# One transfer with an outermost dimension of two, replaced by two of 64 partitions

## The chip, the cores and the metric

The kernel runs on one core of a Trainium2 chip. What is measured is the device time of one execution in microseconds. A kernel is timed in several runs; the median counts. One more execution is recorded by the hardware profiler, and all rows below come from that one.

## What is computed

Four sequences of 576 tokens and eight heads of 64 go through causal attention whose scores get a decay term, and the result goes through two feed-forward layers. Cut to what matters:

```python
scores = np.matmul(q, k.transpose(0, 1, 3, 2)) / np.sqrt(D)      # B=4, H=8, S=576, D=64
cum = np.cumsum(np.log(np.clip(f, 0.0001, 1.0)), axis=-1)
decay = cum[:, :, :, None] - cum[:, :, None, :]
scores = np.where(causal, -1000000000.0, scores + decay)
attn = softmax(scores)
x = np.matmul(attn, v)                    # to 2304 tokens x 512
h = x @ w_in;  x = (h * clip(h + 3, 0, 6) / 6) @ w_out       # first layer, d_ff = 2048
h = x @ w_in2; g = 0 if h <= -1, (h + 1)**2 / 4 in the middle, h if h >= 1
out = g @ w_out2                          # second layer
```

## The kernel before

Attention is cut into jobs. A job of kind "two" takes the first 256 queries of two heads of one sequence; the other 320 queries of a pair of heads are three jobs: two of kind "one" (one head, 256 queries) and one of kind "last". The last job is a tile of 128 partitions: partitions 0 to 63 hold the last 64 queries of the first head, partitions 64 to 127 those of the second. There are 16 such tiles. For each job `u_load` issues the transfers two jobs ahead (k into kraw, q into qraw, the decay rows into dec), `u_split` (one job ahead) lets GpSimd mask the diagonal block of the decay (L569 and L573 for a last tile) and ScalarE and VectorE split k and q into a high and a low part (kk, qh, ql), `u_scores` makes the scores (L630 for a last tile, L655 for the others), VectorE adds the decay and takes the maximum (L606), ScalarE takes the exponential (L612), `u_norm` finishes the sum on ScalarE (L674), and VectorE makes its reciprocal (L675) and the normalised rows (L684). `u_trans` transposes these on TensorE (L697), `u_out` multiplies with v (L739).

The cumulated logarithms lie in the DRAM tensor ncum, one row of 576 numbers for each of 32 heads. dec repeats rows of it over partitions: for jobs "one" and "two" one row over all 128 partitions (L555), for a last tile row r over 64 partitions and row r+1 over the other 64 (L506).

The feed-forward matmuls are mixed with attention. `moe_h` (L833) multiplies by w_in and applies the first function (L840, L841, then L400 and L408 split the result g); `moe_o` (L876) multiplies by w_out, and when a block of tokens is done its sums go through osb (L898, L900) to the DRAM tensor x2d (L902). Blocks 0 and 1 are worked on in two parts each or in one (`OPEN`), so block 0 leaves two partial sums in two tensors x2d, which `moe_x` adds up later. Weights come in raw (wraw, L433), are put together by ScalarE and VectorE (wr, L445 to L456, then L400 and L408) and kept in DRAM (wf, L465) for a second visit. The second layer's matmuls are L833 and L883.

All transfers are issued by SyncE's queue in one order. The order on every engine is written by the kernel itself: `graph` gives each instruction a cost and `schedule` lists, engine by engine, what could start first by these costs; `plan` ties the instructions together in that order. Each engine then works through its list in order. So a change in the number of transfers can move instructions on every engine.

Of the kernel before, what the change touches and what calls it, by code (L numbers as in the profile page):

```python
# [8 lines left out]
F32 = mybir.dt.float32  # L9
# [5 lines left out]
B, H, S, D = 4, 8, 576, 64  # L15
NT, DM, DFF = B * S, H * D, 2048
P = 128
NCH = DFF // P
KD = DM // P
T1 = (512, 512, 512, 256, 512)  # L20
T2 = (512, 512, 512, 512, 256)
NB = len(T1)
NB2 = NB + len(T2)
# [15 lines left out]

SLOTS = (9, 9)  # L40
OPEN = ((0, 0, 8), (1, 0, 8), (1, 8, 16), (0, 8, 16))
LOOK = 5
LAG = 2
GO = 0
# [1 line left out]
LATE = (1, 2.0, 2)  # L46
WRAW = 3
AHEAD = 60000
LEAD = (1, 1, 1, 1, 1, 1)


def plan_weights(visits, slots, more, lag):
# [300 lines left out]
def tile_kernel(  # L353
# [10 lines left out]
    nc = tc.nc  # L364
# [9 lines left out]
    moe = pool("moe", 2)  # L374
    dram = pool("dram", 1, DRAM)
# [10 lines left out]
    att = pool("att", 2)  # L386
    rawp = [att]

    x2d = [dram.tile([DM, NT if x == 0 else T1[0]], F32, name=f"x2d{x}") for x in range(2)]
    wf = [  # L390
        [dram.tile([P, 2, 4, P], F32, name=f"wf{c}_{x}") for x in range(2)]
        for c in range(NCH)
# [1 line left out]
    ncum = dram.tile([B * H, S], F32, name="ncum")  # L394
# [14 lines left out]


    steps = [(j, c) for j, a, e in OPEN for c in range(a, e)]
    for j in range(2, NB2):
        order = range(NCH) if j % 2 else range(NCH - 1, -1, -1)
        steps += [(j, (j >= NB) * NCH + c) for c in order]
    opens = [g for g in range(len(steps)) if g == 0 or steps[g - 1][0] != steps[g][0]]
    closes = [g - 1 for g in opens[1:]] + [len(steps) - 1]
    parts = {g: [steps[x][0] for x in opens[:n]].count(steps[g][0]) for n, g in enumerate(opens)}
    g7 = (NB - 1) * NCH
    where, loads = [], []
    for x in range(2):  # L420
        a, b = plan_weights([c for _, c in steps], SLOTS[x], (16 - SLOTS[x], g7), LAG * x)
# [49 lines left out]
    place, t0 = {}, 0  # L471
    for b, half in ORDER:
# [10 lines left out]
        t0 = place[b, half][1]  # L483
# [14 lines left out]
    def u_load(n):  # L498
        d = jobs[n]
        b, hs, kind, p = d["b"], d["hs"], d["kind"], d["p"]  # L500
        h, nh = hs[0], len(hs)
        r = b * H + h
        if kind == "last":

            d["dec"] = att.tile([P, S], F32, tag="dec", name="dec")
            nc.sync.dma_start(  # L506
                out=d["dec"], in_=ncum[r:r + 2, :].unsqueeze(1).to_broadcast([2, D, S])
            )
            return
        q0, nq, nk = (0, QA, QA) if kind == "two" else (QA, S - QA, S)  # L510
        d["nat"] = n < NATS
# [296 lines left out]
    def moe_x(j):  # L808

        t0, w = FROM[j], WIDTH[j]  # L810
        for k in range(KD):
            x = moe.tile([P, 2, 512], F32R, tag="xt", name="x2", bufs=XT)
            hi, lo = x[:, 0, 0:w], x[:, 1, 0:w]
            full = lo.bitcast(F32)
            if j == NB:
                full, more = (moe.tile([P, 512], F32, tag="wr", name=f"part{y}", bufs=2) for y in range(2))
            nc.sync.dma_start(out=full, in_=x2d[0][k * P:(k + 1) * P, t0:t0 + w])
            if j == NB:
                nc.sync.dma_start(out=more, in_=x2d[1][k * P:(k + 1) * P, t0:t0 + w])
                nc.vector.tensor_tensor(out=full, in0=full, in1=more, op=ALU.add)  # L820
            rounded("p", hi, full)
            rest("v", lo, full, hi)
            xt[j, k] = x
# [126 lines left out]
    n1 = NB * NCH  # L950
# [73 lines left out]
    weights_until(-1)  # L1024


    spans = [(0, 8, 1), (8, 32, 2)] + [(j * NCH, (j + 1) * NCH, j + 1) for j in range(2, NB)]
    cost = [sum(x[0] for x in seq[:n]) for n in range(len(seq) + 1)]
    due = [ends[group(min(j, NB - 1))] for _, _, j in spans]
    goal, n0 = [], pos  # L1030
    for x, (a, e, j) in enumerate(spans):

        n2 = 2 * (e - a)
        left = cost[-1] - cost[n0]
        share = cost[n0] + left * LEAD[x] * (part[e] - part[a]) / (part[g7] - part[a]) if e < g7 else cost[-1]
        aim = max(cost[due[x]], min(share, cost[due[x]] + AHEAD))
        aim = max(aim, cost[n0])
        for y in range(n2):
            goal.append(cost[n0] + (aim - cost[n0]) * (y + 1) / n2)
        while n0 < len(seq) and cost[n0] < aim - 1:  # L1040
            n0 += 1
# [73 lines left out]
```

## Time and profile before

| | |
|---|---|
| time, median of 3 runs | 1024.39 us (1022.07 to 1025.25) |
| the profiled execution: its time | 1025.11 us |
| its span, first to last instruction | 1023.4 us |
| granted TensorE clock, mean over the span | 0.978 of full speed |
| TensorE busy | 994.8 us (97%) |
| VectorE busy | 588.0 us (57%) |
| ScalarE busy | 529.6 us (52%) |
| GpSimd busy | 73.0 us (7%) |

A row of the timeline gives the start in microseconds from the span's start, the duration, the engine (PE is TensorE, PEld its weight loads, DVE VectorE, ACT ScalarE, POOL GpSimd, SPq the queue of SyncE), the line, the operation, output and inputs by name, the shape, the number of instructions in the row and, in brackets, how long the engine stood idle before the row and what ended that. A row of the windows gives for a stretch the length, the busy time of each engine with its number of instructions, then the granted clock, the share of the 16 DMA engines' time in use, and GB/s.

### The profile page before, as it was taken

What the parts mean: (1) busy time and instruction counts of PE and PEld (TensorE: products, weight loads), DVE (VectorE), ACT (ScalarE), POOL (GpSimd) and SP (SyncE); (2) the same over time, 40 slices, a digit from 0 to 9 for tenths busy, and PEclk for the clock granted to TensorE, in tenths of its full rate; (3) what the DMA queues carried; (4) which work ended last, traced back from release to release, by engine and by line L of the source; (5) the groups of instructions that cost most, each with busy time, mean ns of one, the idle gap of its engine ahead of it and who ended that gap; (6) DMA issues with size and microseconds to landing.
All of it is one profiled execution on the core that took longest, in us unless ns stands there. A gap on an engine that the chain in (4) does not pass through costs nothing.

```text
span 1023.4 us, 14617 instructions
## 1 busy us (share of the span) xinstructions
PE 994.8 (97%) x5002; PEld 800.6 (78%) x5002; DVE 588.0 (57%) x1390; ACT 529.6 (52%) x1208; POOL 73.0 (7%) x192
## 2 busy tenths in 40 slices
PE   7889999998999999999999999999999999999998
PEld 5457767876677777778998888878888888888897
DVE  5899876798655555455533669999322322322232
ACT  5889765675655554455532336565333333333343
POOL 1111110110010010000000000201000000000000
PEclk8689999998999999999999999999999999999999
DMA  6766477854466776326636325443100100000010
GB/s 175 213 184 186 130 233 245 284 162 134 100 204 204 243 232 180 111 66 184 233 125 250 124 76 192 176 154 113 42 1 19 48 1 1 27 20 1 1 43 20
DMA packets 69193, 131.39 MB, mean 128 GB/s; under 512 B 11520, under 2 KB 34560, under 8 KB 69120
## 3 DMA queue, kind: packets, MB, share of 16 engines
q1 hardware_dynamic: 69120, 130.47, 41.4%
q8 instruction: 39, 0.64, 0.3%
q14 instruction: 34, 0.28, 0.1%
HBM read 105.20 MB, written 25.24 MB: 127 GB/s over the span
## 4 chain that ended last, share of the span: by engine, by line
PE 80%; DVE 9%; DMA 6%; ACT 2%; issue 2%; SPq 0%; DVEq 0%; POOL 0%; ACTq 0%; POOLq 0%
PE hp L833 33%; PE o L876 17%; PE o L883 17%; PE av L739 4%; PE pt L697 4%; PE sc L655 3%; DMA wraw<-in_w 3%; DMA kraw<-in_k 2%; PE sc L630 2%; DVE wr L453 1%; DVE wr L456 1%; DVE w L408 1%; DVE prob L606 1%; ACT prob L612 1%; DVE wr L446 1%
## 5 line engine op out<-in xcount | busy, mean ns | idle before, releaser
L833 PE MATMUL hp<-xt,w 128*128 128x512 f32 (+1 forms) x960 | 232.6, 382 | 1.1 <-ACT xt L400 0.7
L876 PE MATMUL o<-g,w 128*128 128x512 f32 (+1 forms) x960 | 229.4, 378 | 1.4 <-DVE osb L900 1.4
L833 PE MATMUL hp<-x,w 128*128 128x512 f32 (+1 forms) x960 | 211.5, 368 | 0.5 <-ACT w L400 0.3
L883 PE MATMUL o<-w,g 128*128 128x512 f32 x864 | 210.1, 390 | 0.0
L833 PEld LDWEIGHTS hp<-x,w 128*128 128x128 f32 x960 | 169.2, 188 | 32.7 <-ACT w L400 0.7
L833 PEld LDWEIGHTS hp<-xt,w 128*128 128x128 f32 x960 | 167.0, 192 | 31.8 <-issue 2.4
L876 PEld LDWEIGHTS o<-g,w 128*128 128x128 f32 x960 | 166.0, 189 | 29.7 <-DVE osb L900 1.8
L883 PEld LDWEIGHTS o<-w,g 128*128 128x128 f32 x864 | 161.2, 188 | 32.7
L845 DVE SCALAR_TENSOR_TENSOR u<-hp,u 128x512 f32<-128x512 f32 (+1 forms) x80 | 50.9, 636 | 166.8 <-ACT u L844 166.7
L408 DVE TENSOR_TENSOR g<-u,g 128x512 fp32r<-128x512 f32 (+1 forms) x160 | 102.4, 640 | 56.7 <-ACT g L400 30.3
L400 ACT ACTIVATE g<-u 128x512 fp32r<-128x512 f32 (+1 forms) x160 | 94.5, 591 | 75.8 <-DVE u L845 47.1
L843 ACT ACTIVATE u<-hp 128x512 f32<-128x512 f32 (+1 forms) x80 | 44.3, 554 | 157.9 <-PE hp L833 157.8
L612 ACT ACTIVATE prob<-prob,mx 128x128 f32<-128x128 f32 (+4 forms) x144 | 83.4, 580 | 55.5 <-DVE mx L606 55.3
L841 DVE SCALAR_TENSOR_TENSOR u<-u,hp 128x512 f32<-128x512 f32 (+1 forms) x80 | 50.5, 631 | 90.4 <-ACT u L840 90.1
L840 ACT ACTIVATE u<-hp 128x512 f32<-128x512 f32 (+1 forms) x80 | 44.0, 550 | 90.8 <-PE hp L833 90.6
L697 PE MATMUL pt<-ident,prob 128*128 128x128 f32 (+1 forms) x400 | 71.8, 294 | 13.6 <-DVE prob L684 10.1
L606 DVE CUSTOM_DVE_ANT_0 prob<-sc,dec 128x256 f32<-128x256 f32 (+1 forms) x112 | 58.6, 534 | 37.3 <-PE sc L655 22.5
L400 ACT ACTIVATE pt<-pt 128x512 f32<-128x512 f32 (+3 forms) x160 | 63.4, 433 | 25.2 <-PE pt L697 24.7
L697 PEld LDWEIGHTS pt<-ident,prob 128*128 128x128 f32 (+1 forms) x400 | 51.1, 148 | 32.4 <-DVE prob L684 10.0
L400 ACT ACTIVATE w<-wr 128x512 fp32r<-128x512 f32 x64 | 40.3, 629 | 28.8 <-DVE wr L456 28.5
L739 PE MATMUL av<-pt,vv 128*64 128x320 f32 (+3 forms) x448 | 53.7, 382 | 0.7 <-ACT pt L400 0.7
L445 ACT ACTIVATE wr<-wraw 128x512 f32<-128x512 f32 x64 | 42.9, 670 | 20.8 <-DMA wraw<-in_w 10.2
(69 smaller groups left out, 865.6 us busy)
## 6 DMA issues: line engine op xcount, KB each, us to landing
wraw<-in_w SPq DMA_DIRECT2D x64, 512.0 KB, 4.9
w<-wf SPq DMA_DIRECT2D x40, 512.0 KB, 8.1
wf<-w SPq DMA_DIRECT2D x28, 512.0 KB, 8.7
dec<-ncum SPq DMA_DIRECT2D x45, 256.0 KB, 3.6
kraw<-in_k SPq DMA_DIRECT2D x64, 144.0 KB, 4.1
x2d<-osb SPq DMA_DIRECT2D x22, 256.0 KB, 3.1
vv<-in_v SPq DMA_DIRECT2D x16, 320.0 KB, 7.4
dec<-ncum SPq DMA_DIRECT2D x16, 288.0 KB
```

The lines of the kernel that those rows point to most:

```text
L400: nc.scalar.activation(out=out, in_=in_, func=AF.Copy)
L408: e.tensor_tensor(out=out, in0=in_, in1=hi.bitcast(F32), op=ALU.subtract)
L606: nc.vector.tensor_tensor_reduce(out=py[:, a:e], in0=s, in1=dc, scale=-0.125, scalar=mx[:, 2 * z:2 * z + 1] if x else 3.0e38, op0=ALU.add, ...
L612: nc.scalar.activation(out=py, in_=py, func=AF.Exp, scale=-1.0, bias=mx[:, 2 * z + x:2 * z + x + 1], accum_out=sm[:, z:z + 1],)
L697: nc.tensor.transpose(t[:nk, o:o + P], p[:, c:c + nk], ident)
L739: nc.tensor.matmul(t[y * D:(y + 1) * D, o:nq], lhsT=vv[:, y, c], rhs=rhs, start=c == 0, stop=c == nkc - 1,)
L833: nc.tensor.matmul(hp, lhsT=ws[:, a, k], rhs=x[:, bb, 0:w], start=(k == 0 and a == 0 and bb == 0), stop=(k == KD - 1 and bb == 1),)
L841: nc.vector.scalar_tensor_tensor(out=u, in0=u, scalar=6.0, in1=hp, op0=ALU.min, op1=ALU.mult)
L843: nc.scalar.activation(out=u, in_=hp, func=AF.Relu, bias=0.5, scale=0.5)
L845: nc.vector.scalar_tensor_tensor(out=u, in0=hp, scalar=1.0, in1=u, op0=ALU.max, op1=ALU.min)
L876: nc.tensor.matmul(o, lhsT=ws[:, a, k], rhs=gg[:, bb], start=(n and k % m == 0 and a == 0 and bb == 0), stop=(last and bb == 1 and k % m = ...
L883: nc.tensor.matmul(acc[j][k], lhsT=gg[:, bb, k * P:(k + 1) * P], rhs=ws[:, a].rearrange("p k n -> p (k n)"), start=(n and a == 0 and bb == ...
```

## The change

The transfer of the decay rows for a last tile, one instruction whose outermost dimension has the size two, becomes two instructions of 64 partitions each. The other edits put constants in place that are worked out from `OPEN`; the second x2d tensor becomes 1024 columns wide instead of 512.

```diff
 SLOTS = (9, 9)
 OPEN = ((0, 0, 8), (1, 0, 8), (1, 8, 16), (0, 8, 16))
+OPENED = 1 + max(j for j, _, _ in OPEN)
+HEAD = sum(T1[:OPENED])
+NPART = max(sum(x[0] == j for n, x in enumerate(OPEN) if n == 0 or OPEN[n - 1][0] != x[0]) for j in range(OPENED))
...
-LEAD = (1, 1, 1, 1, 1, 1)
...
-    x2d = [dram.tile([DM, NT if x == 0 else T1[0]], F32, name=f"x2d{x}") for x in range(2)]
+    x2d = [dram.tile([DM, NT if x == 0 else HEAD], F32, name=f"x2d{x}") for x in range(NPART)]
...
-    for j in range(2, NB2):
+    for j in range(OPENED, NB2):
...
             d["dec"] = att.tile([P, S], F32, tag="dec", name="dec")
-            nc.sync.dma_start(
-                out=d["dec"], in_=ncum[r:r + 2, :].unsqueeze(1).to_broadcast([2, D, S])
-            )
+            for y in range(2):
+                nc.sync.dma_start(out=d["dec"][y * D:(y + 1) * D], in_=ncum[r + y:r + y + 1, :].to_broadcast([D, S]))
             return
...
-            if j == NB:
-                full, more = (moe.tile([P, 512], F32, tag="wr", name=f"part{y}", bufs=2) for y in range(2))
+            n = 1 + part_of.get(j - NB, 0)
+            if n > 1:
+                full = moe.tile([P, 512], F32, tag="wr", name="part0", bufs=2)
             nc.sync.dma_start(out=full, in_=x2d[0][k * P:(k + 1) * P, t0:t0 + w])
-            if j == NB:
-                nc.sync.dma_start(out=more, in_=x2d[1][k * P:(k + 1) * P, t0:t0 + w])
+            for y in range(1, n):
+                more = moe.tile([P, 512], F32, tag="wr", name=f"part{y}", bufs=2)
+                nc.sync.dma_start(out=more, in_=x2d[y][k * P:(k + 1) * P, t0:t0 + w])
                 nc.vector.tensor_tensor(out=full, in0=full, in1=more, op=ALU.add)
...
-    spans = [(0, 8, 1), (8, 32, 2)] + [(j * NCH, (j + 1) * NCH, j + 1) for j in range(2, NB)]
+    fresh = [g for g in opens if parts[g] == 0 and g < n1] + [n1]
+    spans = [(a, e, j + 1) for j, (a, e) in enumerate(zip(fresh, fresh[1:]))]
...
-        share = cost[n0] + left * LEAD[x] * (part[e] - part[a]) / (part[g7] - part[a]) if e < g7 else cost[-1]
+        share = cost[n0] + left * (part[e] - part[a]) / (part[g7] - part[a]) if e < g7 else cost[-1]
```

The order moves at more places than the queue. On the other engines it is that of before up to about 140 us of the profile, differs here and there until about 305, and hardly after that. Line numbers in the changed kernel are one to four higher.

**First place: SyncE's queue around 279 us.** dec is the decay rows, wf a 512 KB write of weights kept for later, vv the values, x2d the sums of a finished block. Before:

```order
L526 DMA kraw<-in_k 64x576 x2
L506 DMA dec<-ncum 128x1x576
L539 DMA qraw<-in_q 128x256
L540 DMA qraw<-in_q 128x64
L465 DMA wf_0_98<-w_0_113 128x1024
L493 DMA vv<-in_v 128x2x320
L902 DMA x2d_78<-osb 128x512 x2
```

Now:

```order
L509 DMA dec<-ncum 64x576 x2
L467 DMA wf_0_98<-w_0_113 128x1024
L527 DMA kraw<-in_k 64x576 x2
L495 DMA vv<-in_v 128x2x320
L540 DMA qraw<-in_q 128x256
L541 DMA qraw<-in_q 128x64
L905 DMA x2d_78<-osb 128x512 x2
```

The decay rows are now two instructions and stand ahead of kraw, and the write of wf moved up to stand directly behind them.

**Second place: ScalarE and TensorE around 265 to 272 us**, a last tile (prob_3268, now prob_3274) and the two jobs before it. ScalarE before:

```order
L612 ACTIVATE prob_3236,sum<-prob_3236,mx 128x512
L400 ACTIVATE kk<-kraw 128x576
L674 ACTIVATE sum<-sum 128x2
L612 ACTIVATE prob_3268,sum<-prob_3268,mx 128x576
L674 ACTIVATE sum<-sum 128x1
L400 ACTIVATE qh<-qraw 128x384
L840 ACTIVATE u<-hp 128x512
```

ScalarE now:

```order
L613 ACTIVATE prob_3242,sum<-prob_3242,mx 128x512
L675 ACTIVATE sum<-sum 128x2
L613 ACTIVATE prob_3274,sum<-prob_3274,mx 128x576
L843 ACTIVATE u<-hp 128x512
L675 ACTIVATE sum<-sum 128x1
L402 ACTIVATE kk<-kraw 128x576
```

The conversion of kraw, which waits for a transfer, moved from ahead of the sum to behind both sums. TensorE at the same place, before:

```order
L630 MATMUL sc<-kk,ql 128x512 x2
L630 MATMUL sc<-kk,ql 128x64 x2
L833 MATMUL hp<-xt,w_8_121 128x512 x11
L697 MATMUL pt<-ident,prob_3139 128x128 x2
L697 MATMUL pt<-ident,prob_3236 128x128
```

TensorE now:

```order
L631 MATMUL sc<-kk,ql 128x512 x2
L631 MATMUL sc<-kk,ql 128x64 x2
L836 MATMUL hp<-xt,w_8_121 128x512 x5
L879 MATMUL o_1989<-g,w_5_127 128x512 x2
L698 MATMUL pt<-ident,prob_3145 128x128 x2
L879 MATMUL o_1989<-g,w_5_127 128x512
```

Between the scores and the first transposes (pt) stood eleven matmuls of a feed-forward layer, and now stand seven.

**Third place: VectorE and TensorE around 247 to 252 us**, again a last tile (prob_3008, now prob_3013) and the job before it (prob_2865 and prob_2976, now prob_2870 and prob_2981). VectorE before:

```order
L453 SCALAR_TENSOR_TENSOR wr<-wraw,wr 128x512
L408 TENSOR_TENSOR ql<-qraw,qh 128x384
L456 SCALAR_TENSOR_TENSOR wr<-wraw,wr 128x512
L675 RECIPROCAL rd<-sum 128x2
L606 ISA prob_3008,mx<-sc,dec 128x512
L606 ISA mx 128x1
L684 TENSOR_SCALAR prob_2865<-prob_2865,rd 128x384
L408 TENSOR_TENSOR w_6_128<-wr,w_6_128 128x512
L684 TENSOR_SCALAR prob_2976<-prob_2976,rd 128x512
```

VectorE now:

```order
L458 SCALAR_TENSOR_TENSOR wr<-wraw,wr 128x512
L844 SCALAR_TENSOR_TENSOR u<-u,hp 128x512
L607 ISA prob_3013,mx<-sc,dec 128x512
L607 ISA mx 128x1
L410 TENSOR_TENSOR w_6_128<-wr,w_6_128 128x512
L676 RECIPROCAL rd<-sum 128x2
L607 ISA prob_3013,mx<-sc,dm,mx 128x64
L607 ISA mx 128x1
L410 TENSOR_TENSOR xt<-av,xt 128x320
L685 TENSOR_SCALAR prob_2870<-prob_2870,rd 128x384
L685 TENSOR_SCALAR prob_2981<-prob_2981,rd 128x512
```

The normalisation of the two tiles that are transposed next now has u, the small piece of the last tile's scores and xt ahead of it. TensorE there, before:

```order
L876 MATMUL o_1989<-g,w_3_125 128x512
L876 MATMUL o_1990<-g,w_3_125 128x512 x3
L630 MATMUL sc<-kk,qh 128x64 x2
L630 MATMUL sc<-kk,ql 128x64 x2
L697 MATMUL pt<-ident,prob_2865 128x128
```

TensorE now:

```order
L836 MATMUL hp<-xt,w_6_119 128x512 x3
L631 MATMUL sc<-kk,qh 128x64 x2
L631 MATMUL sc<-kk,ql 128x64 x2
L836 MATMUL hp<-xt,w_6_119 128x512 x6
L698 MATMUL pt<-ident,prob_2870 128x128 x2
```

Nine matmuls of the next feed-forward step now stand ahead of these transposes; the matmuls o that stood there were moved ahead of the scores.

## Rows read from the trace of the kernel before

**Rows 1.** Windows: engines' busy time by stretch, then granted clock, DMA share, GB/s.

```profile
235.00:256.00 21.00, 16.95 (x69) 12.85 (x68) 16.75 (x40) 11.83 (x27) 2.15 (x7) 0.84 0.41 120
256.00:276.00 20.00, 17.53 (x93) 13.15 (x92) 12.16 (x38) 11.83 (x32) 2.10 (x9) 0.91 0.46 113
276.00:295.00 19.00, 17.64 (x91) 13.24 (x90) 9.51 (x24) 9.25 (x22) 0.62 (x3) 1.00 0.48 148
295.00:1010.00 715.00, 714.39 (x3606) 593.15 (x3605) 352.66 (x735) 324.54 (x668) 36.70 (x90) 1.00 0.33 106
```

**Rows 2.** Timeline of TensorE: its waits from 126 to 295 us, and a run.

```profile
137.65 0.33 PE L697 MATMUL pt<-ident,prob 128*128 128x128 f32 x1 [1.77 <-DVE prob L684]
...
240.66 0.63 PE L697 MATMUL pt<-ident,prob 128*128 128x128 f32 x4 [2.00 <-DVE mx L606]
...
251.26 0.96 PE L697 MATMUL pt<-ident,prob 128*128 128x128 f32 x4 [1.02 <-DVE mx L606]
...
266.39 2.78 PE L833 MATMUL hp<-xt,w 128*128 128x512 f32 x11
271.64 1.72 PE L697 MATMUL pt<-ident,prob 128*128 128x128 f32 x7 [2.47 <-DVE prob L684]
...
293.85 1.65 PE L876 MATMUL o<-g,w 128*128 128x512 f32 x6 [1.36 <-DVE osb L900]
```

**Rows 3.** Timeline of VectorE and ScalarE: waits ahead of those of TensorE.

```profile
136.03 0.69 DVE L606 CUSTOM_DVE_ANT_0 prob<-sc,dec 128x512 f32<-128x512 f32 x1 [2.41 <-DMA dec<-ncum]
...
239.13 0.66 ACT L445 ACTIVATE wr<-wraw 128x512 f32<-128x512 f32 x1 [4.79 <-DMA wraw<-in_w]
239.82 0.43 DVE L446 TENSOR_SCALAR wr<-wr 128x512 f32<-128x512 f32 x1 [1.94 <-ACT wr L445]
...
241.62 0.69 DVE L408 TENSOR_TENSOR w<-wr,w 128x512 fp32r<-128x512 f32 x1 [1.10 <-ACT w L400]
...
268.87 0.69 DVE L606 CUSTOM_DVE_ANT_0 prob<-sc,dec 128x512 f32<-128x512 f32 x1 [3.47 <-DMA dec<-ncum]
...
269.46 0.68 ACT L400 ACTIVATE kk<-kraw 128x576 fp32r<-128x576 f32 x1 [3.21 <-DMA kraw<-in_k]
...
293.10 0.69 DVE L900 TENSOR_SCALAR osb<-o 128x512 f32<-128x512 f32 x1 [2.11 <-DMA x2d<-osb]
```

**Rows 4.** Timeline: weights issued behind decay rows; decay rows issued, and first read.

```profile
229.29 0.40 SPq L433 DMA_DIRECT2D wraw<-in_w  x1
...
259.45 0.55 SPq L506 DMA_DIRECT2D dec<-ncum  x1
...
268.80 0.24 POOL L569 TENSOR_SCALAR_AFFINE_SELECT dm<-dec 128x64 f32<-128x64 f32 x1 [5.28 <-DMA dec<-ncum]
```

**Rows 5.** Groups by line: busy us, mean ns, idle us before and its releaser.

```profile
L569 POOL TENSOR_SCALAR_AFFINE_SELECT dm<-dec 128x64 f32<-128x64 f32 x16 | 4.0, 250 | 146.0 <-DMA dec<-ncum 146.0
```

**Rows 6.** The chain of waits: start us, length us, what.

```profile
262.02 7.34 DMA kraw<-in_k
...
286.21 6.77 DMA x2d<-osb
```

**Rows 7.** DMA issues of the whole run: count, KB each, median us to landing.

```profile
wraw<-in_w SPq DMA_DIRECT2D x64, 512.0 KB, 4.9
...
dec<-ncum SPq DMA_DIRECT2D x45, 256.0 KB, 3.6
kraw<-in_k SPq DMA_DIRECT2D x64, 144.0 KB, 4.1
x2d<-osb SPq DMA_DIRECT2D x22, 256.0 KB, 3.1
```

**Rows 8.** DMA issues of the first 126 us alone.

```profile
kraw<-in_k SPq DMA_DIRECT2D x6, 144.0 KB, 2.9
```

**Rows 9.** Windows: the microsecond after the decay rows of 259.45 began to move.

```profile
261.00:262.00 1.00, 1.00 (x13) 0.77 (x10) 0.88 (x3) 1.00 (x5) 0.00 (x0) 1.00 0.18 54
```

**Rows 10.** Line L526: duration ns min/median/max, first and last start us.

```profile
L526 SPq DMA_DIRECT2D kraw<-in_k x80: 471/587/650, 9.0 to 479.6; - x80
```

## Prediction

> **What bounds the kernel now.** I read the windows first. TensorE is the engine that works almost all the time, so what the change can give is what TensorE loses while it waits or runs at the lower clock. From 295 to 1010 us it loses nothing: 714.39 busy of 715.00 at a granted clock of 1.00 [rows 1]. Whatever ends earlier before 295 therefore ends the program earlier by as much. Between 126 and 295, where the transfers that are changed are issued, TensorE is idle in four places: 1.77 us at 137.65 [rows 2], and by the windows 4.05 in 235:256, 2.47 in 256:276 and 1.36 in 276:295, together 9.65 us. Twice the clock falls behind such a stop, from 1.00 to 0.84 over 21 us and to 0.91 over 20 us; since the lower level is half of the higher (1.2 against 2.4 GHz), the share that is missing is time lost: 0.16 x 21 = 3.4 and 0.09 x 20 = 1.8 us [rows 1]. All that can be won is 9.65 + 5.2 = 14.9 us.
>
> The timeline then says who stops TensorE [rows 2]: the transposes L697 wait for VectorE at 137.65, 240.66, 251.26 and 271.64, and the second layer of matmuls L876 at 293.85. One step further back [rows 3] stand transfers. At 136.03 and 268.87 VectorE itself sat idle 2.41 and 3.47 us until the decay rows of a last tile had landed. At 239.13 ScalarE had waited 4.79 us for raw weights, and VectorE 1.94 and 1.10 us behind it. At 269.46 ScalarE had waited 3.21 us for kraw; at 293.10 VectorE 2.11 us for a write of x2d.
>
> These five have one thing in common. The decay rows of a last tile are issued at 259.45 and used at 268.80, 9.35 us later [rows 4]; over all 16 of them GpSimd stood 146.0 us, 9.1 each, waiting for them [rows 5]. And a transfer issued just behind one is late too: the weights issued at 229.29 [rows 4] reach ScalarE at 239.13, 9.8 us, where 4.9 is the median; kraw takes 7.34 us at 262.02 against a median of 4.1, x2d 6.77 at 286.21 against 3.1 [rows 6, 7]. While the decay rows travel almost alone, the queue moves 54 GB/s [rows 9]: 288 KB at that rate take 5.5 us, and 0.18 x 16 is about three DMA engines at work. So the one transfer uses a few of the sixteen engines, and what follows waits on those few.
>
> The Trainium skill, "DMA: Bandwidth & Descriptors", section "Rules for kernel authors", says that an outermost dimension smaller than 16 confines a transfer to at most that many engines; the 54 GB/s agree with it. The same section speaks against this change: two transfers to disjoint halves of the partitions are not worth the trouble, since both spread over the same engines and one follows the other; one transfer of 128 partitions is advised. By that rule alone the halves would land no earlier and the time would stay at 1024.4. The trace has the case that decides between them: 64 partitions x 576, 144 KB, as kraw, landed in 2.9 us before the first of the slow transfers [rows 8].
>
> **The parts, costed.** *Two transfers for one.* Sixteen instructions become 32. A 64-partition issue takes 0.587 us of the queue [rows 10], so what is queued behind (vv, raw weights, the next kraw) is issued up to 0.6 us later, at most 9.4 us of queue in all. For the weights behind the one at 228.6 this is 229.3 + 0.6 + 4.9 = 234.8, against 239.13 now; ScalarE was ready at 239.13 - 4.79 = 234.34 and VectorE at 237.88, so the cost lies under VectorE's work. Nothing is charged.
>
> *Landing.* No row shows a 64-partition transfer that repeats one source row. From below: 2.9 us (kraw undisturbed) + 0.6 for the second issue = 3.5. From above: 9.35, no better than now. I take 4.1 + 0.6 = 4.7, the loaded median of the same shape. Then each stop is followed.
>
> (a) At 126.6 + 4.7 = 131.3 the rows are there before VectorE wants them at 136.03 - 2.41 = 133.6. The 1.77 us go. Bounds 0 and 1.77.
>
> (b) 235 to 256. VectorE's waits of 1.94 and 1.10 us for the weights go, 3.04 in all. That does not give TensorE back all its 4.05 idle and 3.4 clock, because VectorE is the late one there and, as the third pair of order rows shows, its order changes: the normalisation that the transposes wait for comes behind three more instructions (u, the small prob, xt), an estimate of 1.5 us from the 0.4 to 0.7 us of VectorE's rows [rows 3]. TensorE for its part gets nine matmuls of the first layer ahead of these transposes, 9 x 0.25 = 2.3 us of work (2.78 us for 11 in [rows 2]). So TensorE reaches the point of 251.26 us earlier by 3.04 - 1.5 + 2.3 = 3.8 us. Bounds: 1.5 (the nine matmuls only fill a wait that stays) and 7.4 (idle and clock both).
>
> (c) 256 to 276. The rows would land at 264.2, VectorE asked for them at 265.4; kraw at 262.02 + 4.1 = 266.1, ScalarE asked at 266.25. Both fit, with a margin of about 1 us and none. In the new order ScalarE does not convert kraw ahead of the sum that the transposes wait for, so that margin is not needed; but TensorE has seven matmuls between scores and transposes where it had 11, 1.0 us less of cover, against 2.47 to be removed and 3.47 that VectorE gets. I take the idle time and the clock, 2.47 + 1.8 = 4.3. Bounds 1.5 and 4.3.
>
> (d) 293.85. The x2d write was late by 6.77 - 3.1 = 3.7 us, more than the 2.11 that VectorE waited. But the new order puts a 512 KB write of weights (wf) straight behind the decay rows and ahead of kraw and x2d. I count nothing; bounds 0 and 1.36.
>
> *The rest of the diff.* The new names come to the old values: OPENED 2, NPART 2, the same spans and steps, LEAD was all ones. The second copy of x2d becomes 1024 columns wide, read and written in the same 2 KB rows, and it is read in the stretch where TensorE loses 0.6 us in 715. Nothing.
>
> Sum: 1.8 + 3.8 + 4.3 + 0 = 9.9 us. The profiled execution took 1025.11 us, 0.7 above the median, its span 1023.4: it becomes 1015.2, and the median 1024.4 - 9.9 = **1014.5 us**.
>
> **The rivals.** *Smaller gain (15 in 100):* the stops go, but VectorE stays the late one in (b) and the clock falls as before in (c): 1.8 + 1.5 + 2.5 = 5.8, 1018.6 us. For it: VectorE is busy 16.75 of 21 us in 235:256. *Larger (13 in 100):* (d) goes as well and the clock never falls, 14.9 us, 1009.5. For it: no stop of TensorE in 126 to 295 lacks a late transfer ahead of it. *No change (11 in 100):* the halves land as late as the whole, because a source row that is repeated is what is slow, or because each half goes through the same few engines and one follows the other; then only the later issues remain, under the cover shown above, and 1024.4 stays. The second of these is what the Trainium skill's rule on halves, quoted above, would do here. Against both: the 2.9 us of kraw [rows 8], and the other decay rows, repeated over 128 partitions, which land in 3.6 us [rows 7]. *Slower (7 in 100):* the new order is the cause. Between 140 and 305 us transposes stand nearer to the scores that they come from, as in (c), 1.0 us less cover each time; a stop like that of (c) costs 4.3 with the clock that follows. If the removed stops give only (a) back and two new ones arise, the time is 1024.4 - 1.8 + 8.6 = 1031.2; from the second new stop on it is slower. Against it: the order of before, made in the same way, has such stops only behind late transfers.
>
> **Numbers.** The likeliest case has 54 in 100 and its own range of 1012 to 1017.5. A measurement of this kernel tells about 0.3%, 3.1 us, from no change. Faster by more: 54 + 15 + 13 = 82 in 100; within: 11; slower: 7. The range of 1009 to 1022 reaches from all that can be won to the smaller gain with room, and leaves out no change and slower, 18 in 100.
>
> **What would show it.** The decay rows' first reader on GpSimd waits under 80 us in all instead of 146.0; the halves land in under 5.5 us of the first issue; raw weights and kraw behind them in 4 to 5. TensorE's idle time from 126 to the end of attention's tight part falls from 9.65 to about 3 us, and the clock there stays above 0.93. The long rest has the same length, within 1 us. The prediction is wrong if the halves take 8 us or more, if transposes wait for VectorE with no transfer ahead of that wait, or if the wait for weights or kraw stays where it was.

## The result and the profile after

| | before | after |
|---|---|---|
| median, 4 runs of each on one chip | 1023.63 us (1022.07 to 1025.25) | 1010.19 us (1008.89 to 1011.59) |
| the profiled execution: its time, its span | 1025.11, 1023.4 us | 1011.59, 1009.8 us |
| TensorE busy | 994.8 us | 993.5 us |

The ratio is 0.9869 with a 95% interval of 0.9844 to 0.9893: 13.4 us faster, where 9.9 us were forecast. TensorE is busy for about as long as before: what is gone is for the most part time in which it waited, 28.6 us of the span before and 16.3 after. The clock gave time back too, as the windows below show, but not in this sum, because the changed kernel's profiled execution ran its first 126 us at a lower clock than that of before (0.82 against 0.86; see the last section).

The windows of the changed kernel, for the stretches of [rows 1] (the starts and ends of the same work have moved by a few us):

```profile
126.00:140.00 14.00, 14.00 (x75) 11.01 (x75) 10.36 (x30) 8.74 (x24) 1.93 (x8) 1.00 0.85 244
140.00:235.00 95.00, 94.56 (x489) 74.08 (x488) 79.28 (x189) 62.02 (x141) 9.82 (x29) 1.00 0.73 233
235.00:256.00 21.00, 19.99 (x105) 14.19 (x103) 20.26 (x53) 15.70 (x40) 1.63 (x6) 1.00 0.39 116
256.00:276.00 20.00, 19.98 (x107) 14.94 (x107) 13.55 (x39) 12.71 (x33) 2.81 (x11) 1.00 0.54 165
276.00:295.00 19.00, 19.00 (x99) 15.27 (x99) 11.81 (x34) 12.35 (x31) 1.47 (x6) 1.00 0.65 226
295.00:1000.00 705.00, 704.38 (x3558) 585.71 (x3555) 344.24 (x708) 316.61 (x646) 36.02 (x84) 1.00 0.31 104
```

The first busy column is TensorE's. In 235:256 it was 16.95 of 21 us and is 19.99; in 256:276 it was 17.53 of 20 and is 19.98. The clock, the third number from the end, was 0.84 and 0.91 there and is 1.00. The long last stretch lacks 0.62 us, as it lacked 0.61 before, so what ends earlier by 295 is kept to the end.

All waits of TensorE from 126 to 295 us that are left (sum, times, longest, in us):

```profile
PE sc L631 <- DVE mx L607: 1.0, 1, 1.0
PE sc L656 <- DVE mx L607: 0.4, 1, 0.4
```

The five stops of [rows 2] are gone. The longer of the two waits that are left stood there before as well, and it stays now that the transfers are on time:

```profile
PE sc L630 <- DVE mx L606: 0.8, 1, 0.8
```

Gone is also the wait of VectorE that stood behind the first stop, as its row for the same work shows; it waits for the scores now, 0.27 us, and no longer 2.41 us for dec [rows 3]:

```profile
134.56 0.69 DVE L607 CUSTOM_DVE_ANT_0 prob<-sc,dec 128x512 f32<-128x512 f32 x1 [0.27 <-PE sc L631]
```

The decay rows of the last tile that [rows 4] showed, and the group of GpSimd's masks that read them first (busy, mean ns, idle before):

```profile
252.97 1.10 SPq L509 DMA_DIRECT2D dec<-ncum  x2
...
257.29 0.24 POOL L570 TENSOR_SCALAR_AFFINE_SELECT dm<-dec 128x64 f32<-128x64 f32 x1
```

```profile
L570 POOL TENSOR_SCALAR_AFFINE_SELECT dm<-dec 128x64 f32<-128x64 f32 x16 | 5.2, 324 | 55.1 <-DMA dec<-ncum 55.1
```

From the first issue to the mask are 257.29 - 252.97 = 4.3 us, where it was 9.35; the median over the 16 tiles, worked out from their rows in the same way, is 4.0, where it was 9.4. (These are times to the mask, which can start later than the rows land; only 13 of the 16 masks waited for them in the changed kernel.) GpSimd's wait fell from 146.0 us [rows 5] to 55.1. In the microsecond in which the two halves travel, the queue moves 152 GB/s and not 54 [rows 9]:

```profile
254.00:255.00 1.00, 1.00 (x12) 0.60 (x10) 0.88 (x3) 0.97 (x3) 0.00 (x0) 1.00 0.42 152
```

The DMA issues of the whole run (count, KB each, median us to landing) show what else came earlier. The first block is the changed kernel; the second has the rows of before that [rows 7] left out:

```profile
wraw<-in_w SPq DMA_DIRECT2D x64, 512.0 KB, 4.2
w<-wf SPq DMA_DIRECT2D x40, 512.0 KB, 5.2
wf<-w SPq DMA_DIRECT2D x28, 512.0 KB, 4.5
...
kraw<-in_k SPq DMA_DIRECT2D x64, 144.0 KB, 3.2
x2d<-osb SPq DMA_DIRECT2D x22, 256.0 KB, 3.4
vv<-in_v SPq DMA_DIRECT2D x16, 320.0 KB, 3.6
dec<-ncum SPq DMA_DIRECT2D x32, 144.0 KB, 3.2
```

```profile
w<-wf SPq DMA_DIRECT2D x40, 512.0 KB, 8.1
wf<-w SPq DMA_DIRECT2D x28, 512.0 KB, 8.7
...
vv<-in_v SPq DMA_DIRECT2D x16, 320.0 KB, 7.4
```

The transfers wf, w and vv are not rewritten by the change, and they land sooner. The two blocks do not rest on the same transfers, though: in the kernel before, the profile tells the landing of 6 of the 28 wf, 7 of the 40 w and 3 of the 16 vv only, and of 16 of the 64 raw weights. The same ones in the changed kernel, worked out from the trace, have medians of 4.4 us for wf (8.7 before), 5.0 for w (8.1), 4.2 for vv (7.4) and 4.7 for the raw weights (4.9). The raw weights that can be compared were hardly late; what went are the few waits in which ScalarE stood for weights and for kraw, shown here before and then after:

```profile
ACT wr L445 <- DMA wraw<-in_w: 9.6, 2, 4.8
...
ACT kk L400 <- DMA kraw<-in_k: 3.8, 2, 3.2
```

```profile
ACT wr L447 <- DMA wraw<-in_w: 0.6, 1, 0.6
```

x2d, whose rows in [rows 6] show one of 6.77 us, had a median of 3.1 and has 3.4.

To see where the 13.4 us came from, the start of the n-th of TensorE's 5002 matmuls, counted from 0, is set side by side. The old-order kernel is the first experiment below; its matmuls stand in the order of before. In the changed kernel the order differs in places, which shifts work of some tenths of a us from one stretch to the next.

| matmul | before | after | old order | stretch since the row above: after, old order against before |
|---|---|---|---|---|
| 600 | 135.49 | 136.20 | 133.74 | +0.7, -1.8 (from the start) |
| 650 | 148.19 | 146.49 | 143.45 | -2.4, -3.0: term (a) |
| 1100 | 235.09 | 233.18 | 230.32 | -0.2, 0.0 |
| 1200 | 261.54 | 254.47 | 253.13 | -5.2, -3.6: term (b) |
| 1300 | 283.73 | 272.17 | 271.27 | -4.5, -4.1: term (c) |
| 1350 | 295.60 | 282.17 | 281.51 | -1.9, -1.6: term (d) |
| last | 1018.90 | 1005.71 | 1004.90 | +0.2, +0.1 |

The sum over all stretches is -13.2 in these two executions, and the four terms alone are -14.0.

### The profile page after: what moved, and what is told of

It reads as the page before. It is cut to its first block, busy times and chain, and to the rows that moved or that the text cites. A ratio compares the mean times of both kernels' runs of the same rounds, so it can differ in the third digit from the quotient of the medians.

```text
span 1009.8 us, 14636 instructions
## 1 busy us (share of the span) xinstructions
PE 993.5 (98%) x5002; PEld 800.7 (79%) x5002; DVE 587.5 (58%) x1390; ACT 529.6 (52%) x1208; POOL 74.3 (7%) x192
## 4 chain that ended last, share of the span: by engine, by line
PE 86%; DVE 9%; issue 2%; ACT 1%; DMA 1%; SPq 0%; DVEq 0%; ACTq 0%
PE hp L836 35%; PE o L879 18%; PE o L886 17%; PE av L740 5%; PE pt L698 4%; PE sc L656 3%; PE sc L631 2%; DVE wr L455 2%; PE sc L646 2%; DVE w L410 1%; DVE wr L458 1%; DVE wr L452 1%; DMA kraw<-in_k 1%; DVE wr L448 1%; PE dc L550 1%
## 5 line engine op out<-in xcount | busy, mean ns | idle before, releaser
L740 PEld LDWEIGHTS av<-pt,vv 128*64 128x64 f32 x448 | 30.9, 145 | 27.6 <-issue 4.5
```

The costliest lines, as they stand in the source:

```text
L740: nc.tensor.matmul(t[y * D:(y + 1) * D, o:nq], lhsT=vv[:, y, c], rhs=rhs, start=c == 0, stop=c == nkc - 1,)
```

## The experiments

Each kernel starts from the changed kernel. Ratios are to the kernel before, with 95% intervals; the times are medians. The theory from the prediction: the one transfer of outermost size two uses few DMA engines, so it is late itself and makes late what follows. The rival with the most behind it after the result: the new order of the instructions makes the gain, or part of it.

### Fast halves in the order of before

The planner is shown one transfer of 128 partitions in place of the two, so every engine's list is that of before, and the second half is put in right behind the first when the lists are written.

```diff
+TAILS, WIDE = set(), {}
...
+    ops = [i for i in ops if i.name not in TAILS]
...
+        if i.name in WIDE:
+            ins += [x for x in map(operand, WIDE[i.name].ins) if x]
+            outs = [(x[0], 0, P, *x[3:]) for x in outs]
...
+            tail = WIDE.get(ops[k].name)
+            if tail is not None:
+                row += [sets.pop(a.regref) for a in tail.ins if getattr(a, "regref", None) in sets]
+                row.append(tail)
...
```

> Two transfers of 64 partitions as in the changed kernel, but on every engine the order of the kernel before (the two halves stand where the one transfer stood). Theory 1, the transfer: the slow transfer and what waited behind it cause the four stops of TensorE, the new order little of the gain. Then the stops at 137, 240, 271 and 293 us shrink here too and the time is 1010 to 1015 us; in 235 to 256 VectorE gives back its 3.0 us of waiting. Theory 2, the order: the gain comes mostly from nine matmuls ahead of the transposes, the conversion of kraw behind the sum and the like. Then the time is 1018 to 1024 and the stops at 251 and 271 remain.

Measured: 1010.74 us, ratio 0.9889 (0.9867 to 0.991), the changed kernel's time. All of TensorE's waits from 126 to 295 us, then the window of term (b):

```profile
PE pt L710 <- DVE mx L619: 0.9, 1, 0.9
PE sc L643 <- DVE mx L619: 0.8, 1, 0.8
```

```profile
235.00:256.00 21.00, 19.22 (x98) 14.15 (x98) 18.25 (x47) 14.97 (x38) 2.60 (x9) 0.92 0.37 100
```

The new order is not the cause of the gain as a whole. It makes a small part of it. The two waits left here are those of the same matmuls that waited 0.84 us at 249.60 and 1.02 at 251.26 in the kernel before. So the stop at 251.26, one of the five of [rows 2], does not come from a late transfer: with fast halves and the old order it stays, 0.93 us, and the clock is 0.92 in 235:256. In the new order this stop is gone and the clock is 1.00; term (b) is 5.2 there and 3.6 here. In the medians, 1010.74 and 1010.19 us, a part of 1 to 2 us cannot be told from noise.

### Halves that are each confined again

The same instructions in the same order as in the changed kernel; only the source of each half is written with an outermost dimension of two, and the same 64 rows of the same numbers are fetched.

```diff
-                nc.sync.dma_start(out=d["dec"][y * D:(y + 1) * D], in_=ncum[r + y:r + y + 1, :].to_broadcast([D, S]))
+                nc.sync.dma_start(
+                    out=d["dec"][y * D:(y + 1) * D],
+                    in_=ncum[r + y:r + y + 1, :].unsqueeze(1).to_broadcast([2, D // 2, S]),
+                )
```

> The changed kernel in its own order with two transfers of 64 partitions, but the source of each written with an outermost dimension of two (2 x 32 x 576). Theory 1: each half is confined to a few engines again, the decay rows land about 9 us after the first issue, 54 GB/s while they move, and time 1018 to 1025. Theory 2: the order is unchanged, so 1009 to 1012. If a repeated source row or 64 partitions mattered and not the outermost dimension, also 1009 to 1012.

Measured: 1029.32 us, ratio 1.0073 (1.0046 to 1.0099), slower than before and 4 us above the range that was expected. TensorE's waits from 126 to 560 us, GpSimd's masks, and a microsecond in which the halves travel almost alone:

```profile
PE pt L701 <- DVE prob L688: 7.9, 2, 4.3
PE pt L701 <- DVE mx L610: 3.9, 1, 3.9
PE o L882 <- DVE osb L906: 1.9, 1, 1.9
```

```profile
L573 POOL TENSOR_SCALAR_AFFINE_SELECT dm<-dec 128x64 f32<-128x64 f32 x16 | 4.9, 309 | 159.4 <-DMA dec<-ncum 130.8 <-DMA wraw<-in_w 11.2 <-DMA w<-wf 10.7
```

```profile
263.00:264.00 1.00, 1.00 (x12) 0.63 (x8) 0.93 (x4) 0.97 (x4) 0.00 (x0) 1.00 0.14 46
```

One number in an access pattern is worth 19.1 us. The transposes L701 wait for VectorE again and the matmuls L882 (those of L876 in the kernel before) for osb, as in [rows 2], and the queue is at 46 GB/s. So it is neither the number of instructions nor their 64 partitions nor the repeated source row that makes the halves fast, but how the access pattern begins.

### How much of it is needed

The same edit with 4 and with 8 in place of 2 (`[4, D // 4, S]`, `[8, D // 8, S]`).

> The changed kernel and its order, the source of each half with an outermost dimension of four. Theory 1, the number of engines follows the outermost dimension: both halves together need about half of the 5.5 us of the confined form, the queue moves about 108 GB/s, the rows land in 5 to 7 us, and the time lies between the changed kernel and the form with two: 1011 to 1020 us. If there is a threshold instead (few engines for any such form): 1026 to 1031.

> The same with an outermost dimension of eight. Theory 1: about 1.4 us of movement for both halves, the rows land in about 4 us, 1009 to 1012 us. With a threshold: 1026 to 1031.

Measured: 1009.62 us, ratio 0.9865 (0.985 to 0.9879), with 4, which is below the range expected for it; 1009.60, 0.9863 (0.9849 to 0.9876), with 8. The masks' group and a microsecond of the transfer, with 4:

```profile
L573 POOL TENSOR_SCALAR_AFFINE_SELECT dm<-dec 128x64 f32<-128x64 f32 x16 | 4.0, 247 | 102.1 <-DMA dec<-ncum 102.1
```

```profile
252.00:253.00 1.00, 1.00 (x12) 0.73 (x8) 0.93 (x3) 1.00 (x4) 0.00 (x0) 1.00 0.28 88
```

And with 8:

```profile
L573 POOL TENSOR_SCALAR_AFFINE_SELECT dm<-dec 128x64 f32<-128x64 f32 x16 | 4.9, 309 | 69.1 <-DMA dec<-ncum 69.1
```

```profile
253.00:254.00 1.00, 1.00 (x13) 0.71 (x10) 0.94 (x4) 0.97 (x4) 0.00 (x0) 1.00 0.45 168
```

| outermost dimension of each half | DMA share, GB/s in that microsecond | first issue to mask, median of 16 | time |
|---|---|---|---|
| 2 | 0.14, 46 | 11.3 us | 1029.32 us |
| 4 | 0.28, 88 | 7.4 us | 1009.62 us |
| 8 | 0.45, 168 | 5.2 us | 1009.60 us |
| 64 (the change) | 0.42, 152 | 4.0 us | 1010.19 us |
| (before: the whole, 2) | 0.18, 54 | 9.4 us | 1023.63 us |

The rate about doubles with the dimension from 2 to 4 and from 4 to 8. The 152 GB/s of the change are not slower than the 168: its halves began to move 0.2 us into that microsecond. The Trainium skill, "DMA: Bandwidth & Descriptors", section "Rules for kernel authors", says that a dimension of c below 16 confines a transfer to at most c engines; these rows agree, since 0.14, 0.28 and 0.45 of sixteen engines are 2.2, 4.5 and 7.2 (the share takes in the whole of each packet that begins in the microsecond, so it can read a little over).

The landings say the same. Each is told by updates of a semaphore, and counted in the traces they are 16 for every transfer of the changed kernel, but 3 for one with an outermost dimension of 2 (the whole of before, and the halves), 5 with 4 and 9 with 8: always one more than the dimension.

The whole of before moves no faster than the two halves with 2. The DMA packets by queue in the microsecond of [rows 9] (packets, MB, share of 16 engines) show why it read 54 GB/s:

```profile
q1 hardware_dynamic: 20, 0.05, 12.8%
q14 instruction: 1, 0.01, 5.3%
```

One packet there belongs to another queue. The 20 of the transfer, 2304 bytes each, are 46 GB/s, and 0.128 x 16 is two engines; the "about three" of the prediction counted that packet in.

The time does not follow the landing: 7.4 us cost nothing that can be measured. For the rows themselves there is a reason in the prediction's term (a): they are needed some 7 us after the first issue (133.6 - 126.6 = 7.0). What is issued behind them is late by less as well: with 4, ScalarE waits 2.1 us for weights and 0.4 for kraw, where it waited 9.6 and 3.8 before. How the cost of before divides between the two is the matter of the next two experiments.

### A confined transfer behind the fast halves

Here the decay rows come fast, and a transfer of the old form into an unread DRAM tensor is issued straight behind them. So what is queued behind the decay rows is held up as before, while the rows themselves are on time.

```diff
...
+    dump = dram.tile([P, S + D], F32, name="dump")
...
+            nc.sync.dma_start(out=dump[:, 0:S], in_=ncum[r:r + 2, :].unsqueeze(1).to_broadcast([2, D, S]))
...
```

> The changed kernel and its order; straight behind the two halves a further transfer of the old form (outermost dimension two, 128 x 576, 288 KB, to a DRAM tensor that nobody reads). It adds work that the result does not need. Theory 1a, what follows is held up: the decay rows land in 3 to 4 us as now, but weights, kraw and x2d behind them take 7 to 10 us, and the stops of 240, 271 and 293 us or others like them return: 1015 to 1022. Theory 1b, only the lateness of the decay rows themselves counts: 1010 to 1012, and only VectorE's waits for weights grow.

Measured: 1020.58 us, ratio 0.9984 (0.9965 to 1.0003): 10.4 us above the changed kernel. TensorE's waits from 126 to 295 us, the masks' group, and ScalarE's row for weights:

```profile
PE sc L667 <- ACT pt L409: 5.1, 2, 3.1
PE o L890 <- DVE osb L914: 1.8, 1, 1.8
PE pt L709 <- DVE mx L618: 1.6, 1, 1.6
...
```

```profile
L581 POOL TENSOR_SCALAR_AFFINE_SELECT dm<-dec 128x64 f32<-128x64 f32 x16 | 4.9, 304 | 54.1 <-DMA dec<-ncum 54.0
```

```profile
238.34 0.66 ACT L454 ACTIVATE wr<-wraw 128x512 f32<-128x512 f32 x1 [4.52 <-DMA wraw<-in_w]
```

The masks wait 54.1 us, as in the changed kernel, so the decay rows are on time; yet ScalarE waits 4.52 us for weights where it waited 4.79 before [rows 3], and TensorE stops again near four of the five places of [rows 2]. Two of these stops have another last link: the scores L667 wait for ScalarE, which comes late from waits for weights and kraw. The transfer adds bytes and takes the queue's engines for the time that the old one took; it does not tell bytes from engines. But holding up what stands behind costs most of the gain without any late decay rows.

### Late decay rows alone

The halves are fast and nothing is added to the queue; GpSimd, behind the masks of each last tile, runs 22 (then 14) more masks over dec whose condition always holds, so they change nothing and VectorE waits for them. The planner does not see them.

```diff
...
+            for _ in range(22):
+                nc.gpsimd.affine_select(
+                    out=dec[:, 0:W4], in_=dec[:, 0:W4], compare_op=ALU.is_ge, fill=NEG, base=0,
+                    pattern=[[1, W4]], channel_multiplier=1,
+                )
...
```

> The changed kernel and its order and transfers; behind the two masks of each last tile GpSimd runs 22 further masks on the decay rows that change nothing (about 0.24 us each, 5.3 us), so VectorE gets the rows 5 to 6 us later while the queue is undisturbed. GpSimd's other work of those jobs is later too. Theory 1a, what follows in the queue is held up and that costs most: 1011 to 1015 us, with stops of TensorE near 137 and 265 us only. Theory 1b, the lateness of the rows themselves is the cause: 1017 to 1024.

Measured: 1024.36 us, ratio 1.0011 (0.9999 to 1.0023). That is about the top of the range for late rows as the cause, but the masks took longer than had been reckoned, so the rows were ready some 12.4 us after the issue at the first tile, 3 us later than before:

```profile
128.94 7.54 POOL L584 TENSOR_SCALAR_AFFINE_SELECT dec<-dec 128x64 f32<-128x64 f32 x22
...
136.51 0.69 DVE L620 CUSTOM_DVE_ANT_0 prob<-sc,dec 128x512 f32<-128x512 f32 x1 [5.38 <-POOL dec L584]
...
138.13 0.47 PE L711 MATMUL pt<-ident,prob 128*128 128x128 f32 x1 [4.76 <-DVE prob L698]
```

VectorE waits 5.38 us and TensorE 4.76, where they waited 2.41 and 1.77 before. The kernel therefore says that 3 us more of lateness cost much, and not what the lateness of before cost. With 14 masks the median from issue to ready rows is 9.4 us, that of before:

> As the run with 22 further masks on GpSimd, with 14. The 22 took 7.5 us in one place, so the rows came some 12.4 us after their issue, 3 us later than in the kernel before; 14 take 4.8 us, which brings them to about 9.2 us after the issue, as before, with the queue undisturbed. If the lateness of the rows themselves counts by its length: the stops near 137 and 265 us return at 1.5 to 3 us each and the time is 1013 to 1018 us. If what follows in the queue is the whole cause: 1010 to 1012. If GpSimd's other work held up VectorE in the run with 22: 1020 or more here too.

Measured: 1014.5 us, ratio 0.9919 (0.9894 to 0.9943), 4.3 us above the changed kernel. Its waits from 124 to 560 us:

```profile
PE pt L711 <- DVE prob L698: 4.2, 3, 2.5
PE sc L644 <- DVE mx L620: 1.2, 1, 1.2
PE sc L669 <- DVE mx L620: 0.2, 1, 0.2
```

The lateness of the rows is worth about 4 us, and the transfers held up behind them about 10; together 14.7 against the 13.4 of the whole change. The two need not add up, and each may be a little large: both hit the same stops in part, the extra masks also delay GpSimd's other work (in the first five tiles the rows were ready 10.1 to 14.2 us after the issue, where before they were in use after 9.4 to 11.3), and the extra transfer adds bytes.

### Which of the sixteen tiles count

The confined form (2) for the last tiles of the first sequence alone, and, in another kernel, for those of the third and fourth, which are issued from about 313 us on. The edit is that of the latter; the former has `b == 0` in place of `b >= 2`:

```diff
-                nc.sync.dma_start(out=d["dec"][y * D:(y + 1) * D], in_=ncum[r + y:r + y + 1, :].to_broadcast([D, S]))
+                nc.sync.dma_start(
+                    out=d["dec"][y * D:(y + 1) * D],
+                    in_=ncum[r + y:r + y + 1, :].unsqueeze(1).to_broadcast([2, D // 2, S] if b >= 2 else [D, 1, S]),
+                )
```

> The changed kernel and its order; the last tiles of sequences 2 and 3 (issued from about 316 us on, eight of the 16) have the source with an outermost dimension of two, the others are as in the changed kernel. Theory, the loss is a matter of place: after 300 us TensorE has work ahead and a late transfer costs nothing: 1009 to 1012 us. Otherwise, if each slow transfer costs its share: about half of the 19 us by which the form with two in all places was slower, 1018 to 1021.

> The same with only the last tiles of sequence 0 (issued at about 127, 145, 170 and 199 us) in the form with an outermost dimension of two. By place: the stop at 137 us returns (3 to 5.5 us with that form), the ones at 145 to 199 us cost nothing: 1013 to 1017 us. By share: a quarter of 19, 1015.

Measured: 1008.64 us, ratio 0.9856 (0.9832 to 0.988), with the later eight slow; 1014.41, 0.9912 (0.9893 to 0.9931), with the first four slow. GpSimd waits 107.1 us in the former, and TensorE has no stop from it:

```profile
L573 POOL TENSOR_SCALAR_AFFINE_SELECT dm<-dec 128x64 f32<-128x64 f32 x16 | 5.9, 370 | 107.1 <-DMA dec<-ncum 107.1
```

In the latter TensorE waits once more, 3.3 us, for the transposes of the first sequence:

```profile
PE pt L701 <- DVE prob L688: 3.3, 1, 3.3
...
```

So the eight slow tiles after 295 us cost nothing, as the long stretch of [rows 1] promised, and the first four cost 4.2 us. By equal shares the first four would cost 4.8 of the 19.1, so that run alone does not tell place from share; the run with the later eight does.

### The width of x2d, and the old order with confined halves

The second x2d tensor at its old width:

```diff
-    x2d = [dram.tile([DM, NT if x == 0 else HEAD], F32, name=f"x2d{x}") for x in range(NPART)]
+    x2d = [dram.tile([DM, NT if x == 0 else T1[0]], F32, name=f"x2d{x}") for x in range(NPART)]
```

> The changed kernel with the second x2d tensor 512 columns wide as before. All theories: no difference to the changed kernel, 1009 to 1012 us; the instruction order is the same on every engine.

Measured: 1009.97 us, ratio 0.9874 (0.9851 to 0.9897): the width is worth nothing, as was forecast. Last, the order of before (the first experiment's edit) with both halves confined:

```diff
...
+                nc.sync.dma_start(out=d["dec"][y * D:(y + 1) * D], in_=ncum[r + y:r + y + 1, :].unsqueeze(1).to_broadcast([2, D // 2, S]))
...
```

> Order of the kernel before on every engine, two transfers of 64 partitions, the source of each with an outermost dimension of two. Tells why the changed order with such halves took 1029 us, more than the kernel before. If the new order is more sensitive to a late transfer: 1021 to 1026 us here, as the kernel before. If two confined halves one behind the other are worse than one confined whole: 1027 to 1032.

Measured: 1033.14 us, ratio 1.0094 (1.0077 to 1.011); first issue to mask 11.1 us. That is above both ranges that were expected. Two confined halves are worse than one confined whole in either order, so the 1029.32 above is not the new order's doing. Why they land later than the whole (11.1 and 11.3 against 9.4 us to the mask) is shown in part: together they move at the rate of one whole, 46 GB/s, as they would on the same two engines, and the second is issued 0.6 us after the first. The rest of the 1.7 to 1.9 us stays open. The confined halves took 3.8 us longer here than in the new order, but the intervals of the two ratios overlap, so it is not shown that one order bears late transfers better.

## Why the prediction was right, and where it was off

**The bound.** Right. The long rest kept its length (0.62 against 0.61 us lost), and all of the gain arose before 295 us.

**Landing.** 4.7 us estimated, 4.0 measured to the mask. The shape's row (kraw, 2.9 us undisturbed) was the better guide than its loaded median of 4.1, which was loaded by the transfers that the change removed.

**The rule on halves.** The Trainium skill's advice in "DMA: Bandwidth & Descriptors", section "Rules for kernel authors", that two halves of the partitions are not worth it, rests on both forms using all engines; the 13.4 us of this change and the 19.1 us between halves of 64 and of 2 show that this is to be looked at first. The row of the 54 GB/s told it in advance, though it held one packet that was not the transfer's: it was two engines and 46 GB/s, and 288 KB at that rate take 6.4 us, not 5.5.

**(a)** 1.77 forecast, 2.4 measured (3.0 with the order of before). The stop went as said, and 0.6 us more came with it. In the order of before, two smaller waits of 0.2 us each in the same stretch went too, which the step had not listed; in the new order one of 0.4 us stands there, so its 0.6 is not traced to a wait.

**(b)** 3.8 forecast, 5.2 measured. With the order of before it is 3.6: VectorE's waits for weights go, and with them the stop of 2.00 us at 240.66 and half of the clock's loss (0.84 to 0.92 over 21 us, 1.7 us). It is luck in part that 3.6 is close to the 3.04 of VectorE's waits, the first part of the term: by the windows it is 4.05 - 1.78 = 2.3 of idle time and 1.7 of clock. The stop at 251.26 stays in that order, so the step was wrong to count it with those that have a late transfer ahead. The new order removes it, and the rest of the clock's loss with it. The correction for the new order, -1.5 + 2.3 = +0.8, measured 5.2 - 3.6 = +1.6; its reason, nine matmuls ahead of those transposes, fits, but no run changes them alone. What was mis-sized is the clock's share of 3.4 us, which had been left to the upper bound of 7.4. It is 1.00 in this stretch with the new order and 0.92 in the one profile with the old one.

**(c)** 4.3 forecast, 4.5 measured (4.1 in the order of before). Idle time and clock both came back.

**(d)** 0 forecast, 1.9 measured: the step that failed. It held that the 512 KB write of wf behind the decay rows would delay x2d. But wf stands ahead of x2d in the order of before too, as the rows of the first place show, so this was no reason to set the gain at nothing; and behind fast rows it is not late. In the changed kernel it is issued at 269.56 us and lands 3.8 us later, before the two x2d writes of 274.90 and 275.37, which land in about 3.0 where 6.77 stood in [rows 6]. The DMA issues of 269 to 273 us and of 274.5 to 275.7:

```profile
wf<-w SPq DMA_DIRECT2D x1, 512.0 KB, 3.8
```

```profile
x2d<-osb SPq DMA_DIRECT2D x2, 256.0 KB, 3.0
```

The bound of 1.36, the stop itself, was nearly the right answer, as the old order's 1.6 says too.

**The sum.** 9.9 forecast, 13.4 measured, close to the rival that gave 14.9 and 1009.5 us. The rival's two conditions both came true: (d) went, and the clock no longer fell. By the windows, idle time fell from 9.65 to 1.03 us and the 5.2 us of clock came back, 13.8 in all; what is left of the 14.9 is the wait for scores. The rival's reason was not quite right: at 251.26 it is the new order, not a transfer, that ended the stop. The range held the time; the likeliest case's own range (1012 to 1017.5) did not. The two terms that make up most of the miss are (d), at 1.9 us, and (b), which left out the clock, at 1.4. Holding to a zero for (d) was the worse of the two, since its stop had a late transfer ahead of it like the others.

**What would show it.** GpSimd's wait 55.1 us (under 80); halves within 4.0 us (under 5.5); weights and kraw 4.2 and 3.2 us (4 to 5 forecast; kraw was faster); TensorE's idle time in the four places 0.00 + 1.01 + 0.02 + 0.00 = 1.03 us (about 3 forecast, from 9.65); clock 1.00 (above 0.93). None of the three signs that the prediction is wrong appeared.

**The rivals.** No change: refuted by the halves' landing and by the confined halves. Slower by the new order: refuted, since the old order with fast halves has the same time within the noise. The prediction treated the late rows and what is held up behind as one thing; the experiments part them, about 4 and 10 us, neither of them exactly.

## What to carry to other kernels

Read the outermost dimension of every access pattern that repeats a row, not only its size in bytes: where it is small, the rate of the queue in a quiet microsecond shows it (46 GB/s here). In this kernel the bill fell mostly on the transfers queued behind. Cost such a fix from the stops in which the late transfers end, and count each stop whose releaser is one of them, also where a third transfer stands between; a stop that only waits for a busy engine, as that at 251.26, may stay. Past a certain speed nothing more is to be had: 7.4 us to the first reader were as good as 4.0 here, where the rows had a slack of some 7 us.

## What was not expected of the hardware

A transfer confined to few engines made others late that are bigger and issued on their own: the same wf went from 8.7 to 4.4 us, w from 8.1 to 5.0, vv from 7.4 to 4.2 when it went. Masks of GpSimd that read 0.24 us each in single rows took 7.54 us for 22 in a row, 0.34 each. Two confined halves in one queue were read 1.7 to 1.9 us later than one confined whole of the same bytes, at the same 46 GB/s; the second issue explains 0.6 of it. The landing of a confined transfer is told by fewer updates of its semaphore, 3, 5 and 9 for outermost dimensions of 2, 4 and 8, against 16. And the start of the run differs from one execution to the next: the 600th matmul began at 135.49, 136.20 and 133.74 us in the three kernels of the table above, and the windows give a granted clock of 0.86, 0.82 and 0.89 for their first 126 us, before the first of the decay rows in question is issued (126.6 and 127.2 us in before and after). One profile each does not tell more; it is why the terms were read from the differences between rows of the table and not from the rows alone.
